# Reordering VectorE in the attention stage of a Performer-attention + MoE kernel, and starting the first expert weights two steps later

## The chip, the cores and the metric

The kernel runs on one core of a Trainium2 chip. The metric is the device time of one execution in microseconds (us), the median over runs. One execution was also taken by the hardware profiler; its span starts and ends with the program's instructions and is a little shorter than the execution's device time.

Five engines have a queue of instructions each and run side by side: PE (TensorE, matrix products), DVE (VectorE), ACT (ScalarE), POOL (GpSimd) and SP (SyncE, which here only issues transfers). Within a queue instructions go strictly in the order of the program.

## The reference

```python
# attention with random features: q, k, v are (2, 8, 576, 64), omega is (128, 64)
scale = 1 / sqrt(sqrt(64))
def phi(x):                       # x = q * scale or k * scale
    proj = einsum('bhsd,md->bhsm', x, omega)
    sq = sum(x * x, -1) / 2
    h = proj - sq
    h = h - max(h, -1)
    return exp(h) / sqrt(128)
kv = einsum('bhsm,bhsd->bhmd', k_p, v); z = sum(k_p, axis=2)
out = (q_p @ kv) / (q_p @ z + 1e-6)
# then x (1152 tokens x 512) goes through a mixture of 4 experts of width 1024
# (relu(x @ w1[e]) @ w2[e], weighted by normalised probabilities), and through
# h = x @ w_in (512 x 2048); (h * cos(h)) @ w_out (2048 x 512)
```

## The kernel before, in words

**Two streams of work.** The attention is done by pairs of heads: 2 batches x 4 pairs give `NPR` = 8 pairs of 512 tokens each, and one more "tail" that holds the last 64 tokens of every head. A loop `for s in range(NPR + 3)` (line 1257) runs the pairs as a software pipeline. The dense work (experts and the last two layers) is a Python generator `stream`, cut into quanta of 6 or 12 matmuls. `dense_quanta` (L1186) lets one quantum into the loop at four places of a step, but only from step `first` = 6 on. Before step 6 the loop holds attention alone. After the loop the rest of the stream runs by itself.

**One step of the loop.** What stands in step `s`, in the order in which it is written out (each engine keeps this order):

- `kv_of(s - 1)`: 8 matmuls of features of keys with v (tile `kv`, L1074), added to the tail's share on DVE (L1078);
- `turn_phi(s - 1)`: the features of queries `phq` are turned by PE (`tq`, L1087) and copied out of PSUM to `pT`, one half by ACT (L1090), one by DVE (L1092);
- `put_x` of pair `s - 2`: PE turns the attention result `xs` (`tx`, L1035), ACT writes its high part `xh` (L1047), DVE the low part `xl` = value - `xh` (L1049);
- `features` of queries of pair `s` and then of keys of pair `s + 1`: PE projects (`pj_q`, `pj_k`, L985). DVE sums the squares (L992), scales the sum (L993), takes the maxima of the two projections (L998, twice) and makes the bias `nb_q` or `nb_k` (L1003, L1006). ACT takes 8 exponentials with this bias (`phq`, `phk`, L1011);
- `norms_ahead`: POOL squares the next queries and keys (L941) and halves the row three times by adding (L945), into `x2`;
- `turn_ahead(s + 1)`: PE turns the next queries and keys (`tp_q`, `tp_k`, L958), and they are copied out of PSUM: `xT_q` on DVE (L969), `xT_k` on ACT (L967);
- `nums(s - 1)`: PE forms numerators and denominators (`num`, L1103), DVE divides (L1023 to L1027) into `xs`;
- transfers of later pairs on SP's queue (`load_k`, `load_q`, `load_v`).

**The first weights.** The eight pieces of weights that the first expert needs first are read in the loop: `load_a(0, u, "p")` for four pieces of `w1` (`p0` to `p3`, buffers `ra_..`), and `load_v2(0, u)` for four of `w2` (`v0` to `v3`, buffers `rv`). Each is split into a high part (ACT, L129, 128x1024) and a low part (POOL, L134, two instructions). One piece is fetched per step from step 0 on (L1318), and its split comes about two steps later (`wait(2)`). The raw pieces share two buffers (pool `raw`), so a fetch waits until POOL has split the piece before the last one, and SP's queue stands behind that wait.

**PSUM.** All PSUM tiles rotate through 8 banks; a matmul into a new tile waits until the last reader of the bank's earlier tile is done.

Of the kernel before, what the change touches and what calls it, by code (L numbers as in the profile page):

```python
# [13 lines left out]
ALU = mybir.AluOpType  # L14
# [12 lines left out]
def performer_moe_kernel(ctx, tc, q, k, v, omega, probs, w1, w2, w_in, w_out, out):  # L27
    nc = tc.nc
# [336 lines left out]
    def advance(under):  # L365

        for g in list(under):
            if next(g, under) is under:
                under.remove(g)
# [504 lines left out]
    with tc.tile_pool(name="at1", bufs=1) as at1, tc.tile_pool(name="at2", bufs=2) as at2:  # L874
# [63 lines left out]
        def norms_ahead(nm, t):  # L938

            x2 = at2.tile([P, 2 * R, D], F32, tag=f"x2{nm[0]}", name=f"x2_{nm}")  # L940
            nc.gpsimd.tensor_tensor(out=x2, in0=t, in1=t, op=ALU.mult)  # L941
            w = D
            while w > 8:
                w //= 2
                nc.gpsimd.tensor_tensor(  # L945
                    out=x2[:, :, 0:w], in0=x2[:, :, 0:w], in1=x2[:, :, w : 2 * w], op=ALU.add
                )
            sqs[nm] = x2[:, :, 0:w]

        def turn(nm, t, pieces=1):  # L950

            n = R // pieces
            tps = []
            for z in range(pieces):
                tp = bank(f"tp_{nm}_{z}")[:, : n * P]
                tps.append((slice(z * n * P, (z + 1) * n * P), tp))
                for i in range(n):
                    nc.tensor.transpose(  # L958
                        tp[:, i * P : (i + 1) * P], t[:, 2 * (z * n + i) : 2 * (z * n + i) + 2, :], ident
                    )  # L960

            def copy(x=None, x2=None, act=True):
                if x is None:
                    x = at2.tile([P, R * P], F32, tag=f"xT{nm[0]}", name=f"xT_{nm}")
                for z, (c, tp) in enumerate(tps):
                    if act and z == (nm[0] == "q"):
                        nc.scalar.activation(x[:, c], tp, ACTF.Copy)  # L967
                    else:
                        nc.vector.tensor_copy(out=x[:, c], in_=tp)  # L969
                    if x2 is not None:  # L970
                        nc.scalar.activation(x2[:, c], tp, ACTF.Square)
                return x

            return copy

        def features(nm, turned, phi, squares=None):

            nb = at2.tile([P, 2 * R], F32, tag=f"nb{nm}"[:3], name=f"nb_{nm}")
            pjs = [bank(f"pj_{nm}_{g}") for g in range(2)]
            for i in range(R):  # L980
                c = slice(i * P, (i + 1) * P)
                for z, (x_, y) in enumerate([(turned, ws)] + [(squares, minus_norm)] * (squares is not None)):
                    for g, pj in enumerate(pjs):
                        r = slice(g * D, (g + 1) * D)
                        nc.tensor.matmul(  # L985
                            pj[:, i * M : (i + 1) * M], x_[r, c], y[r, :],
                            start=z == 0, stop=z == (squares is not None),
                        )
            yield
            three = at2.tile([P, 2 * R, 3], F32, tag=f"th{nm[0]}", name=f"three_{nm}")  # L990
            if squares is None:
                nc.vector.tensor_reduce(out=nb, in_=sqs.pop(nm), op=ALU.add, axis=AX.X)  # L992
                nc.vector.tensor_scalar(  # L993
                    out=three[:, :, 1], in0=nb, scalar1=-SC * SC / 2, scalar2=None, op0=ALU.mult
                )
            for g, pj in enumerate(pjs):
                to = (nb if squares is not None else three[:, :, 0])[:, g : 2 * R : 2]
                nc.vector.tensor_reduce(  # L998
                    out=to, in_=pj.rearrange("p (a m) -> p a m", m=M), op=ALU.max, axis=AX.X,
                    negate=squares is not None,  # L1000
                )
            if squares is None:
                nc.vector.tensor_reduce(  # L1003
                    out=three[:, :, 2], in_=three[:, :, 0:2], op=ALU.add, axis=AX.X, negate=True
                )
                nc.vector.tensor_reduce(out=nb, in_=three[:, :, 1:3], op=ALU.add, axis=AX.X)  # L1006
            yield
            for g, pj in enumerate(pjs):
                for i in range(4):
                    ix = g + 2 * i  # L1010
                    nc.scalar.activation(  # L1011
                        phi[:, ix, :], pj[:, i * M : (i + 1) * M], ACTF.Exp, bias=nb[:, ix : ix + 1]
                    )
                yield
# [16 lines left out]
        def put_x(nm, kk, xs, t0, n):  # L1031

            tp = bank(f"tx_{nm}")
            for i in range(n):
                nc.tensor.transpose(tp[:, i * P : (i + 1) * P], xs[:, i, :, :], ident)  # L1035
            yield
            to, i0 = [], 0
            while i0 < n:
                c, o = divmod(t0 + i0, TC)
                m_ = min(n - i0, TC - o)  # L1040
                d = slice(o * HALF, (o + m_ - 1) * HALF + 1, HALF) if c == 0 else (
                    slice(where(c).start + o, where(c).start + o + m_)
                )
                to.append((as_tiles(tp[:, i0 * P : (i0 + m_) * P]), *(x[:, kk, d, :] for x in x_t)))
                i0 += m_
            for src, xh, xl in to:
                nc.scalar.activation(xh, src, ACTF.Copy)  # L1047
            for src, xh, xl in to:
                nc.vector.tensor_tensor(out=xl, in0=src, in1=xh.bitcast(F32), op=ALU.subtract)  # L1049

# [131 lines left out]

        first = 6
        budget = [0.0]

        def dense_quanta(s, n):  # L1186
            if s < first:
# [4 lines left out]
                next(stream)  # L1192

        DQ = 1.0
        wload = []
        turned = {}

        def q_of(s):
# [24 lines left out]
        warm(1)  # L1223
        q0 = turn("q0", qts[0])
        warm(1)
        turned["k", 0], turned["q", 0] = k0(), q0()
        xkL = at2.tile([P, R * P], F32, tag="pT0", bufs=1, name="xkL")
        x2L = at2.tile([P, R * P], F32, tag="pT1", bufs=1, name="x2L")
        phiL = at1.tile([P, H, M], F32, name="phiL")
# [27 lines left out]
        for s in range(NPR + 3):  # L1257
            if s == 0:
                load_k(3)
                load_q(2)  # L1260
                load_v(1)
            else:
                if s < first:
                    advance(wload)
                dense_quanta(s, DQ)
                kvs = kv_of(s - 1) if s <= NPR else iter(())
                next(kvs, None)
                if s == 1:
                    turn_phi(0)
                    kv_tail(phiL)  # L1270
                next(kvs, None)
                if s >= first:
                    advance(wload)
                dense_quanta(s, DQ)
                if 2 <= s <= NPR:
                    turn_phi(s - 1)
                elif s == NPR + 1:
                    tail_turn_phi()
                px = iter(())
                if 2 <= s <= NPR + 1:  # L1280
                    b, hp = pairs[s - 2]
                    px = put_x(f"{s - 2}", hp, xss.pop(s - 2), b * R, R)
                elif s == NPR + 2:
                    px = tail_put_x()
                next(px, None)
                for _ in px:
                    pass
                fs = []
                if s <= NPR:
                    fs.append(q_features(s))  # L1290
                if s + 1 < NPR:
                    fs.append(k_features(s + 1))
                for f in fs:
                    next(f)
                for f in fs:
                    next(f)
                dense_quanta(s, DQ)
                for f in fs:
                    for _ in f:
                        pass  # L1300
                if s + 1 <= NPR:
                    norms_ahead(f"q{s + 1}", q_of(s + 1))
                if s + 2 < NPR:
                    norms_ahead(f"k{s + 2}", kts[s + 2])
                turn_ahead(s + 1)
                dense_quanta(s, DQ)
                if s <= NPR:
                    nums(s - 1)
                elif s == NPR + 1:
                    tail_nums()  # L1310
                if s + 3 < NPR:
                    load_k(s + 3)
                if s + 2 < NPR:
                    load_q(s + 2)
                if s + 1 < NPR:
                    load_v(s + 1)
            advance(wload)
            if s < 2 * NU:  # L1318
                wload.append(load_a(0, s, "p") if s < NU else load_v2(0, s % NU))
                advance(wload)  # L1320
            if s == 2:
                nc.vector.tensor_reduce(out=psum_, in_=pr, op=ALU.add, axis=AX.X)
            if s == 4:
# [44 lines left out]
```

## Time and profile before

| | us |
|---|---|
| median of 3 runs | 664.62 (662.21 to 665.06) |
| the profiled execution, device time | 663.72 |
| its span | 661.9 |
| PE busy | 651.8 (98%) |
| DVE / ACT / POOL busy | 495.6 / 355.5 / 170.7 |
| first dense matmul of the loop starts at | 64.15 |

A busy PE is not a fast PE: its clock has two levels, and the profile gives the granted clock of each stretch as a share of the full one. In the stretch without dense work (the first 64 us) PE is slower than in the rest or waits; what it waits for there is the matter of the rows below. Times of one execution differ from the median by some tenths of a per cent.

### The profile page before, as it was taken

The numbers are of one execution on the slowest core, as the hardware profiler recorded it, in microseconds if no ns is written. First come the engines' busy times: TensorE is split into PE (matmuls) and PEld (weight loads), VectorE is DVE, ScalarE is ACT, GpSimd is POOL, SyncE is SP. The second block draws the span as 40 slices with busy tenths as digits, with TensorE's granted clock in tenths as the row PEclk, the third lists the DMA queues.
The fourth block names the chain that finished last, engine by engine and source line by source line (L and its number), as shares of the span: only waits on it lengthen the run. The fifth ranks groups of instructions, "written<-read, shape, count | busy, mean of one in ns | idle before, by whom it ended". The sixth has DMA issues, their size and how long they took to land.

```text
span 661.9 us, 9631 instructions
## 1 busy us (share of the span) xinstructions
PE 651.8 (98%) x3495; PEld 565.5 (85%) x3495; DVE 495.6 (75%) x916; ACT 355.5 (54%) x703; POOL 170.7 (26%) x220
## 2 busy tenths in 40 slices
PE   9898999999999999999999999999999999999997
PEld 8898998998888888888888888888999888888887
DVE  6868657778969767679778688698778676497842
ACT  6676655436645445345444254464376884467921
POOL 8768544203333232323333322220000000000000
PEclk9988999999999999999999999999999999999999
DMA  7743212131444533435534344420801000700111
GB/s 188 199 128 96 51 64 63 54 107 64 149 151 147 184 134 128 127 128 159 191 100 147 119 145 161 156 79 17 318 32 33 1 0 24 294 1 1 48 49 48
DMA packets 55439, 70.93 MB, mean 107 GB/s; under 512 B 15200, under 2 KB 40032, under 8 KB 55392
## 3 DMA queue, kind: packets, MB, share of 16 engines
q1 hardware_dynamic: 46800, 40.92, 20.0%
q0 software_dynamic: 8448, 29.37, 13.0%
q8 instruction: 27, 0.44, 0.3%
q14 instruction: 20, 0.16, 0.1%
q10 hardware_dynamic: 144, 0.03, 0.0%
HBM read 55.36 MB, written 14.94 MB: 106 GB/s over the span
## 4 chain that ended last, share of the span: by engine, by line
PE 86%; DVE 6%; ACT 3%; issue 2%; DMA 1%; POOL 1%; ACTq 0%; DVEq 0%; POOLq 0%
PE g L704 43%; PE g L503 5%; PE g_odd L533 3%; PE g_0a L503 2%; PE g_0c L503 2%; PE g_3a L503 2%; PE g_2a L503 2%; PE g_1a L503 2%; PE g_2c L503 2%; PE g_3c L503 2%; PE g_1c L503 2%; PE kv L1074 2%; PE g_0b L503 1%; PE g_0e L503 1%; PE g_0d L503 1%
## 5 line engine op out<-in xcount | busy, mean ns | idle before, releaser
L674 ACT ACTIVATE sth<-h 128x512 fp32r<-128x512 f32 (+1 forms) x114 | 61.0, 551 | 66.4 <-PE g L704 51.5
L248 POOL TENSOR_TENSOR c<-c 128x512 uint32<-128x512 uint32 x32 | 46.7, 1458 | 83.8 <-issue 29.1
L677 DVE SCALAR_TENSOR_TENSOR stl<-h,sth 128x512 fp32r<-128x512 f32 (+1 forms) x72 | 50.3, 717 | 20.9 <-ACT sth L674 20.5
L704 PE MATMUL g<-v3h,sth 128*128 128x512 f32 (+1 forms) x110 | 42.8, 390 | 0.0
L704 PE MATMUL g<-v0h,stl 128*128 128x512 f32 (+1 forms) x110 | 42.6, 387 | 0.1
L704 PE MATMUL g<-v1h,sth 128*128 128x512 f32 (+1 forms) x110 | 42.7, 388 | 0.0
L704 PE MATMUL g<-v2h,sth 128*128 128x512 f32 (+1 forms) x110 | 42.6, 387 | 0.0
L704 PE MATMUL g<-v0h,sth 128*128 128x512 f32 (+1 forms) x110 | 42.6, 387 | 0.0
L704 PE MATMUL g<-v2h,stl 128*128 128x512 f32 (+1 forms) x110 | 42.5, 387 | 0.0
L704 PE MATMUL g<-v1h,stl 128*128 128x512 f32 (+1 forms) x110 | 42.4, 386 | 0.0
L704 PE MATMUL g<-v3h,stl 128*128 128x512 f32 (+1 forms) x110 | 42.4, 386 | 0.0
L704 PE MATMUL g<-v0l,sth 128*128 128x512 f32 (+1 forms) x110 | 42.4, 386 | 0.0
L704 PE MATMUL g<-v1l,sth 128*128 128x512 f32 (+1 forms) x110 | 42.4, 385 | 0.0
L704 PE MATMUL g<-v3l,sth 128*128 128x512 f32 (+1 forms) x110 | 42.4, 385 | 0.0
L704 PE MATMUL g<-v2l,sth 128*128 128x512 f32 (+1 forms) x110 | 42.4, 385 | 0.0
L282 DVE TENSOR_TENSOR stl<-h,sth 128x512 fp32r<-128x512 f32 (+1 forms) x42 | 24.4, 588 | 21.1 <-ACT sth L674 20.7
L1011 ACT ACTIVATE phq<-pj_q,nb_q 128x128 f32<-128x128 f32 x72 | 19.6, 383 | 24.6 <-DVE nb_q L1006 14.7
L403 DVE SCALAR_TENSOR_TENSOR c<-c 128x384 f32<-128x384 f32 (+2 forms) x44 | 25.8, 591 | 9.0 <-ACT c L401 8.8
L233 ACT ACTIVATE c<-c 128x512 f32<-128x512 f32 x32 | 21.1, 660 | 17.1 <-DMA kv_0h<-c 8.8
L232 ACT ACTIVATE c<-c 128x512 f32<-128x512 uint32 x32 | 21.3, 666 | 8.5 <-DMA c<-in_moe_w_in_dram 7.5
L401 ACT ACTIVATE c<-c 128x384 f32<-128x384 f32 (+2 forms) x44 | 24.4, 555 | 1.4
L704 PEld LDWEIGHTS g<-v0h,stl 128*128 128x128 f32 x110 | 20.7, 188 | 4.9 <-DVE stl L677 0.7
(416 smaller groups left out, 1941.2 us busy)
## 6 DMA issues: line engine op xcount, KB each, us to landing
rv<-in_moe_w_dram SPq DMA_DIRECT2D x16, 512.0 KB, 3.8
c<-in_moe_w_in_dram POOLq DMA_DIRECT2D x16, 512.0 KB, 4.2
c<-in_moe_w_out_dram POOLq DMA_DIRECT2D x16, 512.0 KB, 3.8
kt<-in_k_dram SPq DMA_DIRECT2D x8, 256.0 KB, 3.8
qt<-in_q_dram SPq DMA_DIRECT2D x8, 256.0 KB, 4.0
ve<-in_v_dram SPq DMA_DIRECT2D x16, 128.0 KB, 3.8
ra_2as<-in_moe_w_dram SPq DMA_DIRECT2D x8, 256.0 KB, 3.0
ra_3as<-in_moe_w_dram SPq DMA_DIRECT2D x8, 256.0 KB, 3.7
```

Source lines behind the costliest of these rows:

```text
L232: nc.scalar.activation(lw.bitcast(F32), lw, ACTF.Copy, bias=2.0, scale=2.0**-51)
L233: nc.scalar.activation(t.bitcast(F32), hw.bitcast(F32), ACTF.Abs)
L248: nc.gpsimd.tensor_tensor(out=total, in0=t, in1=lw, op=ALU.add)
L282: nc.vector.tensor_tensor(out=dst, in0=x, in1=y, op=ALU.subtract)
L401: nc.scalar.activation(kk, vv, ACTF.Copy, bias=ROUND)
L403: nc.vector.scalar_tensor_tensor(out=vv, in0=kk, scalar=ROUND, in1=vv, op0=ALU.subtract, op1=ALU.subtract)
L503: nc.tensor.matmul(dst, x[:, o], y[:, kk], start=start and n == 0, stop=stop and n == 3 * kn - 1, skip_group_check=reopen,)
L533: nc.tensor.matmul(g, x[:, kk], w[:, :, :, kk, :], start=n == 0, stop=n == 3 * KD - 1)
L674: nc.scalar.activation(hi, src, ACTF.Relu if self.e < E else ACTF.Copy)
L677: nc.vector.scalar_tensor_tensor(out=to, in0=src, scalar=0.0, in1=hi.bitcast(F32), op0=ALU.max, op1=ALU.subtract)
L704: nc.tensor.matmul(g, x, y[:, o : o + w], start=n == 0, stop=n == 3 * FT - 1)
L1011: nc.scalar.activation(phi[:, ix, :], pj[:, i * M : (i + 1) * M], ACTF.Exp, bias=nb[:, ix : ix + 1])
```

## The change

Five edits, all in the attention loop and ahead of it:

1. `features`: the sums of squares are scaled on POOL, in `norms_ahead`, instead of on DVE (L993 goes; a new POOL instruction of 128x8x8 for each of 17 tiles).
2. `turn`: `xT_q` is copied by ACT instead of DVE (except for the first two pairs, which pass `act=False`).
3. `put_x` yields between ACT's `xh` and DVE's `xl`, and the loop puts `xl` behind the maxima and the bias of queries, ahead of those of keys.
4. The first weights are fetched at the end of steps 2 (`p0`), 3 (`p1`), 4 (`p2`), 5 (`p3` and `v0`), 6 (`v1`, `v2`) and 7 (`v3`), instead of one a step in steps 0 to 7.
5. `q0` keeps its copy on DVE by an argument.

```diff
@@ norms_ahead
+            nc.gpsimd.tensor_scalar(
+                out=x2[:, :, 0:w], in0=x2[:, :, 0:w], scalar1=-SC * SC / 2, scalar2=None, op0=ALU.mult
+            )
             sqs[nm] = x2[:, :, 0:w]
@@ turn
-                    if act and z == (nm[0] == "q"):
+                    if act and (z == 0 or nm[0] == "q"):
                         nc.scalar.activation(x[:, c], tp, ACTF.Copy)
                     else:
                         nc.vector.tensor_copy(out=x[:, c], in_=tp)
@@ features
-                nc.vector.tensor_reduce(out=nb, in_=sqs.pop(nm), op=ALU.add, axis=AX.X)
-                nc.vector.tensor_scalar(
-                    out=three[:, :, 1], in0=nb, scalar1=-SC * SC / 2, scalar2=None, op0=ALU.mult
-                )
+                nc.vector.tensor_reduce(out=three[:, :, 1], in_=sqs.pop(nm), op=ALU.add, axis=AX.X)
@@ put_x
             for src, xh, xl in to:
                 nc.scalar.activation(xh, src, ACTF.Copy)
+            yield
             for src, xh, xl in to:
                 nc.vector.tensor_tensor(out=xl, in0=src, in1=xh.bitcast(F32), op=ALU.subtract)
@@ the loop
+        fetched = {2: [("p", 0)], 3: [("p", 1)], 4: [("p", 2)], 5: [("p", 3), ("v", 0)]}
+        fetched.update({6: [("v", 1), ("v", 2)], 7: [("v", 3)]})
...
-        turned["k", 0], turned["q", 0] = k0(), q0()
+        turned["k", 0], turned["q", 0] = k0(), q0(act=False)
...
                 next(px, None)
-                for _ in px:
-                    pass
+                next(px, None)
...
                 for f in fs:
                     next(f)
-                for f in fs:
+                for f in fs[:1]:
+                    next(f)
+                for _ in px:
+                    pass
+                for f in fs[1:]:
                     next(f)
...
-            if s < 2 * NU:
-                wload.append(load_a(0, s, "p") if s < NU else load_v2(0, s % NU))
-                advance(wload)
+            for kind, u in fetched.get(s, ()):
+                wload.append(load_a(0, u, "p") if kind == "p" else load_v2(0, u))
+                next(wload[-1])
```

**VectorE, step 3.** Before, from the addition of `kv` to the bias of queries (`tq`, `tx`, `pj` are PSUM tiles, numbers are the tiles' own):

```order
L1078 TENSOR_TENSOR kv_142<-kv_662,kvL_146 128x2x65
L1092 COPY pT_1_684<-tq_1_679 128x512
L1049 TENSOR_TENSOR xl<-tx_686,xh 128x3x128
L1049 TENSOR_TENSOR xl<-tx_686,xh 128x128
L992 TENSOR_REDUCE nb_q_697<-x_q_606 128x8
L993 TENSOR_SCALAR three_q_719<-nb_q_697 128x8
L998 TENSOR_REDUCE three_q_719<-pj_q_0_698 128x4
L998 TENSOR_REDUCE three_q_719<-pj_q_1_699 128x4
L1003 TENSOR_REDUCE three_q_719<-three_q_719 128x8
L1006 TENSOR_REDUCE nb_q_697<-three_q_719 128x8
```

In the change the same stretch of VectorE's queue reads:

```order
L1079 TENSOR_TENSOR kv_142<-kv_652,kvL_146 128x2x65
L1093 COPY pT_1_674<-tq_1_669 128x512
L995 TENSOR_REDUCE three_q_707<-x_q_597 128x8
L998 TENSOR_REDUCE three_q_707<-pj_q_0_686 128x4
L998 TENSOR_REDUCE three_q_707<-pj_q_1_687 128x4
L1003 TENSOR_REDUCE three_q_707<-three_q_707 128x8
L1006 TENSOR_REDUCE nb_q_685<-three_q_707 128x8
L1050 TENSOR_TENSOR xl<-tx_676,xh 128x3x128
L1050 TENSOR_TENSOR xl<-tx_676,xh 128x128
L995 TENSOR_REDUCE three_k_715<-x_k_603 128x8
```

The two `xl` instructions went from ahead of the maxima of queries to behind their bias, and the scaling is gone.

**ScalarE, from the exponentials of keys in step 2 to those of queries in step 3.** Before (`w02h` is the high part of the weight piece `p1`):

```order
L1011 ACTIVATE phk_553<-pj_k_1_567,nb_k_565 128x128 x4
L967 ACTIVATE xT_k_628<-tp_k_0_621 128x512
L129 ACTIVATE w02h<-ra_1p 128x1024
L1090 ACTIVATE pT_0_677<-tq_0_672 128x512
L1047 ACTIVATE xh<-tx_686 128x3x128
L1047 ACTIVATE xh<-tx_686 128x128
L1011 ACTIVATE phq_695<-pj_q_0_698,nb_q_697 128x128 x4
```

In the change the same stretch of ScalarE's queue reads:

```order
L1011 ACTIVATE phk_544<-pj_k_1_558,nb_k_556 128x128 x4
L970 ACTIVATE xT_q_619<-tp_q_0_609 128x512
L970 ACTIVATE xT_k_621<-tp_k_0_614 128x512
L1091 ACTIVATE pT_0_667<-tq_0_662 128x512
L1047 ACTIVATE xh<-tx_676 128x3x128
L1047 ACTIVATE xh<-tx_676 128x128
L1011 ACTIVATE phq_683<-pj_q_0_686,nb_q_685 128x128 x4
```

The copy of the turned queries came in behind the exponentials of keys, and the split of weights left this step (`p0` is split in step 4 now, `p1` in step 5, `p2` in step 6, `p3` and `v0` in step 7, `v1` and `v2` in step 8).

**SyncE, the fetches of step 5's end and after.** In the change SP's queue has, from the fetch of the last queries on:

```order
L911 DMA qt_3_1067<-in_q_dram 128x2x256
L920 DMA ve_133<-in_v_dram 128x4x64 x2
L160 DMA ra_3p<-in_moe_w_dram 128x4x128 x2
L138 DMA rv_0_1075<-in_moe_w_dram 128x2x512
L920 DMA ve_134<-in_v_dram 128x4x64 x2
L138 DMA rv_1_1228<-in_moe_w_dram 128x2x512
L138 DMA rv_2_1230<-in_moe_w_dram 128x2x512
```

Two fetches of weights stand together twice here; before, a fetch of queries, keys or v stood between any two of the first seven pieces.

## Rows read from the trace of the kernel before

**Rows 1.** Windows: length; PE, PEld, DVE, ACT, POOL busy (instructions); PE's granted clock; DMA.

```profile
33.00:38.00 5.00, 5.00 (x25) 5.00 (x26) 2.25 (x11) 4.58 (x13) 2.73 (x5) 0.50 0.52 148
43.50:52.10 8.60, 8.24 (x86) 7.60 (x85) 6.19 (x19) 5.63 (x17) 4.77 (x6) 1.00 0.34 93
...
64.15:661.90 597.75, 593.59 (x2944) 511.01 (x2944) 448.83 (x780) 314.65 (x575) 123.36 (x144) 1.00 0.31 102
```

**Rows 2.** The timeline, 21 to 32 us, ACT and DVE (start, length, instruction, idle before).

```profile
21.30 2.18 ACT L1011 ACTIVATE phq<-pj_q,nb_q 128x128 f32<-128x128 f32 x8 [2.52 <-DVE nb_q L1006]
...
23.32 2.23 ACT L1011 ACTIVATE phk<-pj_k,nb_k 128x128 f32<-128x128 f32 x8
...
25.32 0.71 ACT L967 ACTIVATE xT_k<-tp_k 128x512 f32<-128x512 f32 x1
...
25.80 1.18 ACT L129 ACTIVATE w02h<-ra_0p 128x1024 fp32r<-128x1024 f32 x1
...
26.75 0.72 ACT L1090 ACTIVATE pT<-tq 128x512 f32<-128x512 f32 x1
...
28.05 0.76 DVE L1049 TENSOR_TENSOR xl<-tx,xh 128x384 fp32r<-128x384 f32 x2 [1.90 <-ACT xh L1047]
...
28.72 0.21 DVE L992 TENSOR_REDUCE nb_q<-x_q 128x8 f32<-128x64 f32 x1
28.96 0.63 DVE L993 TENSOR_SCALAR three_q<-nb_q 128x8 f32<-128x8 f32 x1
29.51 1.28 DVE L998 TENSOR_REDUCE three_q<-pj_q 128x4 f32<-128x512 f32 x2
...
31.02 0.17 DVE L1006 TENSOR_REDUCE nb_q<-three_q 128x8 f32<-128x16 f32 x1
...
31.31 2.18 ACT L1011 ACTIVATE phq<-pj_q,nb_q 128x128 f32<-128x128 f32 x8 [3.29 <-DVE nb_k L992]
```

**Rows 3.** The timeline: the next steps' first exponentials of queries, and the first dense matmul.

```profile
42.30 2.18 ACT L1011 ACTIVATE phq<-pj_q,nb_q 128x128 f32<-128x128 f32 x8 [2.86 <-DVE nb_q L1006]
...
52.94 2.18 ACT L1011 ACTIVATE phq<-pj_q,nb_q 128x128 f32<-128x128 f32 x8 [3.29 <-DVE nb_k L992]
...
62.95 2.18 ACT L1011 ACTIVATE phq<-pj_q,nb_q 128x128 f32<-128x128 f32 x8 [3.20 <-PE num L1103]
...
64.15 0.45 PE L503 MATMUL g<-xh,w02h 128*128 128x384 f32 x1 [0.34 <-ACT phq L1011]
```

**Rows 4.** The timeline on PE: `kv` after a wait, a step's `pj_q` and `num`, `pj_q` later.

```profile
32.51 3.68 PE L1074 MATMUL kv<-ve,phk 128*128 128x65 f32 x16 [1.91 <-ACT phq L1011]
...
47.28 1.16 PE L985 MATMUL pj_q<-ws,xT_q 64*128 64x128 f32 x16
...
50.20 1.90 PE L1103 MATMUL num<-kv,pT 128*128 128x65 f32 x16
...
54.14 2.00 PE L1074 MATMUL kv<-ve,phk 128*128 128x65 f32 x16 [2.04 <-ACT phq L1011]
...
69.56 1.16 PE L985 MATMUL pj_q<-ws,xT_q 64*128 64x128 f32 x16
...
81.31 1.16 PE L985 MATMUL pj_q<-ws,xT_q 64*128 64x128 f32 x16
```

**Rows 5.** Single lines of DVE over the whole run: count, ns shortest/median/longest.

```profile
L993 DVE TENSOR_SCALAR three_q<-nb_q x9: 173/535/966, 9.7 to 93.8; 128x8 f32<-128x8 f32 x9
...
L992 DVE TENSOR_REDUCE nb_q<-x_q x9: 208/208/221, 9.4 to 93.6; 128x8 f32<-128x64 f32 x9
```

**Rows 6.** The chain that ended last, ahead of step 1 (start, length, what).

```profile
9.09 0.33 POOL x_q L945
...
9.70 0.74 DVE three_q L993
```

**Rows 7.** The timeline: a low part on POOL; and the page's transfers (KB, us to landing).

```profile
27.06 2.50 POOL L134 TENSOR_TENSOR w02l<-ra_0p,w02h 128x512 fp32r<-128x512 f32 x2 [3.96 <-DMA ve<-in_v_dram]
...
rv<-in_moe_w_dram SPq DMA_DIRECT2D x16, 512.0 KB, 3.8
```

More of the change, by code (lines that the diff above doesn't have):

```diff
@@ L1184, in performer_moe_kernel @@
         budget = [0.0]
+        wload = []
+        fetched = {2: [("p", 0)], 3: [("p", 1)], 4: [("p", 2)], 5: [("p", 3), ("v", 0)]}
+        fetched.update({6: [("v", 1), ("v", 2)], 7: [("v", 3)]})
         def dense_quanta(s, n):
@@ L1194, in performer_moe_kernel @@
         DQ = 1.0
-        wload = []
         turned = {}
```

## The prediction

> **What bounds the kernel now.** I began with the windows. From the first dense matmul at 64.15 to the end PE is busy 593.59 of 597.75 us at full clock, so little can be won there. Ahead of it lies the attention part, and there a window (33 to 38) calls PE busy at a granted clock of 0.50, that is 1.2 GHz in place of 2.4 [rows 1]. What stands behind 64.15 is a fixed queue of matmuls; it ends earlier by as much as it begins earlier, as long as nothing new makes it wait. The question is what sets 64.15.
>
> It is a loop from step to step. I take the first exponential of queries (`phq`) as the mark of a step: 21.30 and 31.31 [rows 2], then 42.30, 52.94 and 62.95 [rows 3], so steps 1 to 4 take 10.01, 10.99, 10.64 and 10.01 us, 41.65 in all. The timeline of the first of them shows the order of starts [rows 2]: ACT does `phq` for 2.02 (21.30 to 23.32), `phk` for 2.00, then one after the other `xT_k`, the split `w02h`, `pT` and `xh`. Only then can DVE begin `xl` (it had waited 1.90 for ACT), and behind `xl` stand the sum of squares, its scaling and the maxima of queries, whose bias releases the next `phq`; ACT sat idle 3.29 until it came. ACT's jobs and DVE's chain follow each other instead of overlapping. PE is not the limit: the window from 43.50, where a `kv` begins, to 52.10, where the step's last `num` ends, holds a whole step's matmuls and is 8.60 long, 8.24 of it busy, at full clock [rows 1, 4]. PE waits for the exponentials instead: 1.91 us ahead of one `kv`, 2.04 ahead of another [rows 4].
>
> The clock makes it worse. Behind the wait of 1.91 the granted clock is 0.50, and the 16 matmuls of `kv` take 3.68 us, where they take 2.00 elsewhere [rows 1, 4]; that step is the longest of the four.
>
> **The change part by part.** *`xl` behind the queries' bias, and the copy on ACT.* In the new loop, from mark to mark: `phq` 2.02, `phk` 2.00, then `xT_q` stands first on ACT; it takes what `xT_k` took, 0.71 [rows 2]. When it is done, PE projects the queries, 1.16 for `pj_q` [rows 4]. Then come the maxima of queries; from their start to the next `phq` it is 29.51 to 31.31, 1.80 [rows 2]. The sum of squares is done before that, while DVE waits. Together 7.69 us. From step 2 on `xl` stands between the bias of queries and the maxima of keys, so `phk` begins later. From the start of the queries' bias, 0.29 ahead of the mark, DVE needs about 0.1 for itself, 0.67 for `xl` (28.05 to 28.72), 0.24 for the sum (to 28.96), and 1.80 again for the keys' maxima and bias: `phk` starts 2.5 after the mark, not 2.02, which is 0.49 more and makes **8.18 us** [rows 2].
>
> The rest of ACT's work must fit beside that. Between `phk` and the next `phq` stand `xT_q` and `xT_k` (0.48 each by their starts) and `pT` and `xh` (1.30 from the start of `pT` to `xl`), 2.26 of the 3.67 us that PE and DVE need meanwhile; the split, 0.95 by starts, comes back in step 4 and fits too [rows 2]. If it did not, a step with a split would be up to 0.95 longer.
>
> Step 1 has no `xl`: 7.69. Steps 2 to 4 at 8.18 are 24.54. Together 32.2 for 41.65: **-9.4 us**.
>
> *PE in that loop.* Its matmuls, 8.24 busy, stand against 8.18. I count them as just hidden, because the window's busy time includes waits inside merged rows; if 8.60 is the limit, steps 2 to 4 cost 0.42 more each and step 1 0.9, 2.2 us.
>
> *Scaling on POOL.* On DVE the scaling of eight numbers a row took 173 to 966 ns, median 535 [rows 5]; in the loop it goes with the sums above. Ahead of step 1 the first queries' sum waits for POOL, so there the new instruction counts twice (keys, then queries), against 0.74 of scaling on the path [rows 6]. No row shows this instruction. Below it could be next to nothing; above, one of the two instructions of a low part, 1.25 at eight times its columns [rows 7]; the nearest row is the last halving of the sum, 0.33 on the same 64 columns [rows 6], and I take that: 2 x 0.33 - 0.74 = -0.1. The scalings of `k1` and `q1` lie in a busy stretch of DVE and give at least their shortest time, 0.173 each [rows 5], -0.3. **-0.4 us** (-1.0 at nothing, +1.5 at 1.25). In later steps the squares are made a step ahead, which hides the instruction; without that cover two of them would lengthen each step, 0.7.
>
> *Start of the dense part.* The first dense matmul stands behind `num` on PE. From the end of `pj_q` (48.44) to the end of `num` (52.10) PE needs 3.66 [rows 4]. The mark comes 1.80 after the end of `pj_q`, so `num` ends 1.9 behind the mark, where the dense part began 1.20 behind it before (62.95 to 64.15) [rows 3]. **+0.7 us.**
>
> *Weights two steps later.* ACT has the same 8 splits, but they meet a date: `p3` is split in step 7 and used there behind `pj_q`. Counted from the mark of step 6: `phk` is over at 4.5, `xT_q` at 5.0, one evacuation of a dense tile (about like `pT`, 0.48) at 5.5, the high part at 6.7 (1.18), POOL's low part at 9.2 (2.50) [rows 2, 7]. PE, bound by its own queue there, ends `pj_q` of step 7 at 9.95 (11.75 after that of step 6, which is 1.80 ahead of the mark [rows 4]). So about 0.7 us are to spare. **0**; without that cover PE stands for what is missing, 1 to 3 us.
>
> The sum: -9.4 - 0.4 + 0.7 = **-9.1**. The profiled execution took 663.72, its span 661.9; that gives 654.6. The median of the runs, 664.62, is 0.9 above the profiled execution, so I predict **655.5 us**.
>
> **A page weighed against the rows.** The scaling that is removed took 0.63 at 28.96 while POOL's low part ran from 27.06 to 29.56 [rows 2, 7]; the sums of squares never took more than 221 ns in nine cases [rows 5]. So the stretch goes with the scaling and does not pass to the sum that now stands in its place. If it passed, about 0.4 (535 - 173 ns) in four steps and ahead of them, 2 us of the 9.1 would be gone. The Trainium skill (SBUF — State Buffer, section "SBUF: two separate sides") says that VectorE and GpSimd hold one port pair exclusively, which binds VectorE instructions in a two-port mode or with two SBUF inputs, and that the loser waits for the whole instruction. By that rule one-input sums outside such a mode stay free, as the rows say, and the sum stays -9.1.
>
> **The rivals.** *The clock falls as before.* For it: PE has a small gap in every new step, about half a us until `xT_q` is done. Against it: the window from 43.50 has 0.36 without work and a granted clock of 1.00; the fall came behind 1.91 [rows 1, 4]. The longest step shows the price, 10.99 against 10.01, about 1 us; in all four steps 4, so 659.5. The Trainium skill (TensorE: Matmul & The Clock Gate, Part 1, "The HAM clock gate") has the array throttled by default and released by activity; the trace agrees, with 0.50 behind that wait and 1.00 in the dense part. Chance 0.12.
>
> *Smaller terms go against me*: PE's matmuls as the limit (2.2), the stretch passed on (2), a dear POOL instruction (1.9). One or two of them: 657 to 659.5. Chance 0.14.
>
> *The gain is given back*: the dense part starts earlier but waits for its first weights by as much. For it: splits are now packed into steps 4 to 8, two in each of steps 7 and 8, with 0.7 us to spare at one place. Against it: a landing of 3.8 us [rows 7] against steps of 8 to 12. It needs a delay of 6 to 12 us: 661.5 to 667, call it 664. Chance 0.07.
>
> *Slower.* One mechanism: ACT's queue is held by the high part of `v0`. Its fetch waits on SP until POOL has freed the raw buffer of `p2`, split in step 6; ACT reaches it in step 7 ahead of `pT`, `xh` and the next `phq`, and all stand behind it. POOL frees the buffer about 9.5 behind the mark of step 5, and ACT comes 6.7 behind that of step 6, which is some 10 us after it, so 7 us later; the landing takes 3.8 [rows 7], so 3 are to spare. Only a landing of 7 begins to cost, one of 16 eats the gain, and from 20 us on it is slower by 0.5%: 668. Chance 0.03.
>
> **How the numbers follow.** My forecast holds 0.64, with a range of its own from 653.5 to 657. About 0.5%, 3.3 us, is what a measurement of this kernel can tell from no change; below 661.3 is faster. The forecast, the smaller terms and most of the clock's case lie there, 0.88; the gain given back and what is left of the clock's case make 0.08 same; slower is 0.04, with 0.01 from the upper end of the gain given back. The range goes from 652.5, where POOL's instruction costs nothing and the steps are 0.4 shorter, to 660, which takes in the smaller terms and the clock.
>
> **What would show it.** Marks 8.2 us apart in steps 2 to 4, the first dense matmul at about 55, a granted clock of 1.00 in all windows of the loop, no wait of 1.9 for `xh` ahead of `xl`, and ACT's idle time ahead of `phq` down to 1.4 where no split stands. Wrong it would be if a window ahead of 55 shows 0.50, if PE waits in steps 6 to 9 for `w3l` or a `v` piece, or if marks stay 10 apart.

## The result and the profile after

The changed kernel takes **654.9 us** (median; 654.76 to 655.47) where the kernel before took 662.92 in the same runs (662.03 to 665.06): ratio 0.9875, 95% interval 0.9856 to 0.9893, so 1.25% faster. The prediction was 655.5 us, and its sum for the profiled execution 654.6; that execution took 654.85 (span 652.7). The profiled execution of the kernel before, 663.72, lies 0.8 above the median of its runs, so what the two traces differ by (spans 661.9 and 652.7, 9.2 us) is more than the 8.0 us between the medians. One execution of the kernel before, among those that belong to the four "only" kernels below, took 930.53 us at a mean granted clock of 0.654, a slow state of the chip, and is left out of all medians and ratios.

The time came from the loop. In the timeline of the changed kernel, the marks (the first `phq` of a step) and the first dense matmul; rows 2 and 3 answer to them [rows 2, 3]:

```profile
21.22 2.18 ACT L1011 ACTIVATE phq<-pj_q,nb_q 128x128 f32<-128x128 f32 x8 [2.44 <-DVE nb_q L1006]
...
29.07 2.18 ACT L1011 ACTIVATE phq<-pj_q,nb_q 128x128 f32<-128x128 f32 x8 [1.59 <-DVE nb_q L1006]
...
37.16 2.18 ACT L1011 ACTIVATE phq<-pj_q,nb_q 128x128 f32<-128x128 f32 x8 [1.53 <-DVE nb_q L1006]
...
45.26 2.17 ACT L1011 ACTIVATE phq<-pj_q,nb_q 128x128 f32<-128x128 f32 x8 [0.59 <-DVE nb_q L1006]
...
53.35 2.18 ACT L1011 ACTIVATE phq<-pj_q,nb_q 128x128 f32<-128x128 f32 x8 [0.49 <-DVE nb_q L1006]
...
54.96 0.42 PE L503 MATMUL g<-xh,w02h 128*128 128x384 f32 x1
```

Steps 1 to 4 take 7.85, 8.09, 8.10 and 8.09 us, 32.13 in all instead of 41.65. The dense part starts at 54.96 instead of 64.15, 9.19 earlier, and the windows show that it is otherwise what it was: 597.74 us now, 597.75 before [rows 1]. In the stretch 20 to 66 the granted clock is 1.00 throughout; in the same window of the kernel before it was 0.89, with 41.36 us busy. The windows (length; PE, PEld, DVE, ACT, POOL busy; granted clock; DMA), first of the kernel before:

```profile
20.00:66.00 46.00, 41.36 (x373) 39.22 (x374) 34.26 (x109) 30.33 (x98) 32.20 (x44) 0.89 0.47 131
```

and of the changed kernel:

```profile
20.00:66.00 46.00, 45.46 (x464) 43.60 (x461) 33.52 (x110) 37.49 (x120) 38.47 (x59) 1.00 0.45 126
...
54.96:652.70 597.74, 593.39 (x2946) 511.17 (x2945) 445.50 (x773) 318.11 (x579) 132.28 (x157) 1.00 0.32 104
```

What closes the loop now is read in the chain that ended last, here one step of it, from `xl` of step 2 to `xl` of step 3:

```profile
28.95 0.66 DVE xl L1050 x2
29.61 0.13 DVE three_k L995
29.74 1.21 DVE three_k L998 x2
...
31.17 0.17 DVE nb_k L1006
31.34 0.08 DVE rd L1023
...
31.44 1.71 ACT phk L1011 x7
...
33.62 0.49 ACT xT_q L970
...
34.16 1.21 PE pj_q L988 x16
35.37 1.28 DVE three_q L998 x2
...
36.88 0.17 DVE nb_q L1006
37.04 0.66 DVE xl L1050 x2
```

`xh`, `pT` and `phq` are no longer in it; ACT does them beside it. It runs over the copy that the change put on ACT (`xT_q`) and over `xl` ahead of the maxima of keys, as the prediction's sum of 8.18 had it.

### The profile page after: what moved, and what is told of

Same layout as the page of the kernel before. It is cut to its first block, busy times and chain, and to the rows that moved or that the text cites. A ratio compares the mean times of both kernels' runs of the same rounds, so it can differ in the third digit from the quotient of the medians.

```text
span 652.7 us, 9626 instructions
## 1 busy us (share of the span) xinstructions
PE 646.7 (99%) x3495; PEld 561.7 (86%) x3495; DVE 484.9 (74%) x892; ACT 359.3 (55%) x710; POOL 176.9 (27%) x237
## 4 chain that ended last, share of the span: by engine, by line
PE 90%; DVE 5%; issue 2%; ACT 2%; DMA 1%; POOL 0%; DVEq 0%; ACTq 0%; POOLq 0%
PE g L704 44%; PE g L503 5%; PE g_odd L533 3%; PE g_0a L503 2%; PE g_0c L503 2%; PE g_3a L503 2%; PE g_2c L503 2%; PE g_2a L503 2%; PE g_1a L503 2%; PE g_3c L503 2%; PE g_1c L503 2%; PE pj_q L988 2%; PE kv L1075 1%; PE num L1104 1%; PE g_0b L503 1%
```

## The experiments

Each part was run alone on the kernel before ("only"), and each was taken out of the changed kernel ("less"). Time is the median with its range; steps 1 to 4 are the distances of the marks in the profiled execution. The two kernels themselves are in the first two rows; the steps of before are those of the rows ahead of the prediction [rows 2, 3]. Each ratio goes by runs of before in between: their median is 663.30 us for the four "only" kernels, 662.35 for the four "less", 662.26 for the last three.

| kernel | us | ratio to before, 95% | steps 1 to 4 | dense part from |
|---|---|---|---|---|
| before | 662.92 (662.03–665.06) | 1 | 10.01 10.99 10.64 10.01 | 64.15 |
| changed | 654.90 (654.76–655.47) | 0.9875 (0.9856–0.9893) | 7.85 8.09 8.10 8.09 | 54.96 |
| only_order | 654.72 (654.55–655.16) | 0.9873 (0.9853–0.9894) | 7.44 7.86 7.91 7.95 | 55.83 |
| only_weights | 659.62 (659.24–660.33) | 0.9944 (0.9922–0.9966) | 8.82 8.59 9.99 9.98 | 60.11 |
| only_copy | 664.92 (663.34–666.71) | 1.0023 (1.0007–1.0038) | 10.53 10.49 10.47 10.55 | 65.45 |
| only_scaling | 661.25 (659.32–664.31) | 0.9970 (0.9951–0.9989) | 9.33 9.48 9.34 9.43 | 59.89 |
| less_order | 659.87 (659.17–663.71) | 0.9960 (0.9943–0.9977) | 8.88 8.87 9.83 10.68 | 61.03 |
| less_weights | 655.11 (654.55–655.80) | 0.9885 (0.9857–0.9913) | 7.85 8.09 8.09 8.09 | 55.29 |
| less_copy | 654.39 (654.21–654.64) | 0.9874 (0.9846–0.9901) | 7.84 7.84 7.85 7.84 | 54.50 |
| less_scaling | 655.57 (654.81–655.81) | 0.9889 (0.9862–0.9917) | 8.11 8.29 8.29 8.39 | 56.12 |
| clock_fill | 662.04 (661.73–663.55) | 0.9998 (0.9989–1.0007) | 10.00 9.98 9.99 9.99 | 62.87 |
| xl_last | 656.88 (656.14–657.40) | 0.9920 (0.9907–0.9934) | 7.84 8.48 8.48 8.48 | 56.61 |
| pe_more | 657.98 (657.90–658.17) | 0.9935 (0.9923–0.9948) | 8.73 8.74 8.74 8.74 | 58.79 |

**Theory:** the gain is the loop ACT → `xl` → maxima → ACT, which the order of `xl` breaks. **Rival:** it is the work taken off DVE, ACT's splits moved away and the clock, each with its share.

**only_order.** `put_x` (which now yields between `xh` and `xl`) and the loop as in the change, the rest as before:

```diff
+            yield
...
-                for _ in px:
-                    pass
+                next(px, None)
...
-                for f in fs:
+                for f in fs[:1]:
+                    next(f)
+                for _ in px:
+                    pass
+                for f in fs[1:]:
                     next(f)
```

> The kernel before with the third edit alone: xl behind the bias of queries. Theory (the loop ACT, then xl, then maxima was the bound, and the order breaks it): marks about 8.0 to 8.4 us apart, since pj_q no longer waits for the copy of the turned queries (VectorE has it early), ACT's seven jobs with the split (7.4) fit beside it, and the scaling of keys' sums stays on the way to phk; first dense matmul near 56.5, -7.5 us on the kernel before, granted clock 1.00. Rival (work taken off ScalarE and VectorE is what gains): -2 us at most, marks still near 9.5 or more.

This part alone gives the whole gain, 654.72, with the marks closer than I had expected (7.44 to 7.95). In the built program the loop's PSUM tiles have the same banks as in the kernel before up to step 3, so there the order is all that differs. PE is then the limit: in its timeline one `kv` follows the other after 7.85 us, without an idle time ahead of it:

```profile
32.15 1.95 PE L1075 MATMUL kv<-ve,phk 128*128 128x65 f32 x16
...
40.00 1.95 PE L1075 MATMUL kv<-ve,phk 128*128 128x65 f32 x16
```

**only_weights, only_copy, only_scaling.** The weights' schedule alone (`fetched`), the copy alone (`act and (z == 0 or nm[0] == "q")` with `act=False` for `q0`), and the scaling alone:

> The kernel before with the fourth edit alone: first weights two steps later. Theory: the loop stays, ScalarE has 0.95 less in the first two steps and the same later, -1.9 us, and maybe 1 more if one fall of the clock goes. Rival (weights out of the way are the main gain): -5 us or more.

> The kernel before with the second edit alone: xT_q copied by ScalarE. Theory: ScalarE is in the loop, so each step grows by 0.48, +1.9 us, and pj_q comes later. Rival (VectorE is the bound and is relieved by 0.68 a step): -2 us.

> The kernel before with the first edit alone: the scaling of sums on GpSimd. Theory: what the scaling held on the path goes, 0.55, 0.11, 0.54 and 0.45 from its start to the maxima of queries in steps 1 to 4 and about 0.7 once ahead of phk: -2.3 us, nothing in the part ahead of step 1. Rival (the stretch passes to another instruction): 0.

With the weights moved, steps 1 and 2, which lost their splits, fall to 8.82 and 8.59, but a window at 52 to 54 still has PE at 0.50; the gain, 3.7 us, was larger than the 1.9 to 2.9 I had said. One part that I had not counted: without the low part on POOL, the scaling of step 1 takes 0.17 us and not 0.63. The copy alone makes the kernel slower, by 0.07% to 0.38% (1.6 us by the medians): it makes ACT's half of the loop longer, to 10.5 us a step. The scaling alone shortens each step, yet the time fell by 2.1 us only. Its dense part starts at 59.89 after PE waited 1.37 us for ACT, and its clock is down to 0.53 in the window from 60 to 64 (it is 0.50 from 64 to 66 and 1.00 again from 68 on):

```profile
60.00:64.00 4.00, 4.00 (x18) 4.00 (x18) 1.94 (x9) 4.00 (x14) 3.50 (x7) 0.53 0.12 48
```

The rest took 660.8 - 59.89 = 600.9 us instead of 597.75 [rows 1], so 3 us of what the loop gave came back. Alone the three are worth 3.7, -1.6 and 2.1 us; what they are worth beside the order, the next four show.

**less_order, less_weights, less_copy, less_scaling.** The changed kernel without one part each:

> The changed kernel without the third edit: xl again ahead of the maxima of queries. Theory (the order carries the gain): the loop is back with phq 2.02, phk 2.00, xT_q 0.48, xT_k 0.48, pT 0.48, xh 0.8, xl 0.67, sum 0.13 and maxima 1.80, that is 8.9 us a step and 9.8 in the two with a split, 5.4 us slower than the changed kernel, near 660.3. Rival (the other three edits carry it): within 2 us of the changed kernel, near 656.

> The changed kernel with the first weights fetched one a step from step 0 on, as before. Theory: the split fits beside PE's and VectorE's chain (ScalarE still idled 0.5 ahead of phq in the steps that have it), so 0, near 655. Rival: 0.95 in each of the first two steps, 656.8.

> The changed kernel with xT_q copied by VectorE again. Theory by the same chain: pj_q no longer waits for a copy behind phk but for tx, which waits for xs on VectorE, now 0.7 later: marks about 7.9 apart instead of 8.09, -0.6 us, so 654.3 or no difference. Rival (the copy on ScalarE is needed): +0.68 a step, 657.6.

> The changed kernel with the scaling on VectorE again. Theory: the queries' scaling hides in the 0.95 us that VectorE waits for pj_q, but that of the keys' sums stands on the way to phk and costs 0.1 to 0.9 a step: +1 to +2 us, near 656.4. Rival: hidden as well, 0.

Without the order the other parts leave 659.87, so beside them the order is worth 5.0 us: the loop is back, as this kernel's timeline on DVE shows, where `xl` waits for `xh` and the maxima of queries stand behind `xl`:

```profile
36.31 0.76 DVE L1049 TENSOR_TENSOR xl<-tx,xh 128x384 fp32r<-128x384 f32 x2 [1.47 <-ACT xh L1047]
36.98 0.21 DVE L995 TENSOR_REDUCE three_q<-x_q 128x8 f32<-128x64 f32 x1
37.11 1.28 DVE L998 TENSOR_REDUCE three_q<-pj_q 128x4 f32<-128x512 f32 x2
```

In the changed kernel the maxima stand ahead, and wait for PE instead:

```profile
34.18 0.21 DVE L995 TENSOR_REDUCE three_q<-x_q 128x8 f32<-128x64 f32 x1
35.35 1.29 DVE L998 TENSOR_REDUCE three_q<-pj_q 128x4 f32<-128x512 f32 x2 [0.96 <-PE pj_q L988]
...
36.88 0.17 DVE L1006 TENSOR_REDUCE nb_q<-three_q 128x8 f32<-128x16 f32 x1
36.96 0.74 DVE L1050 TENSOR_TENSOR xl<-tx,xh 128x384 fp32r<-128x384 f32 x2
```

Beside the order the weights are worth 0.2 us by the medians, the copy -0.5 and the scaling 0.7 (less than the 1 to 2 us that I expected). The changed kernel was timed in another round; by the ratios it is 0.7, -0.1 and 0.9, and the intervals of all three ratios overlap with the changed kernel's, so the times do not show a gain or a loss for any of the three. The marks are clearer: without the copy all steps take 7.84 and the dense part starts 0.46 earlier; without the scaling on POOL steps take up to 8.39.

**pe_more.** less_copy, with one half of `num` issued twice in the first five pairs:

```diff
-                for r in range(R):
+                for r in list(range(R)) * (2 if i < 5 and h == 0 else 1):
                     nc.tensor.matmul(
                         num[:, r * (D + 1) : (r + 1) * (D + 1)], pT[:, r * P : (r + 1) * P],
```

> The changed kernel without the copy of xT_q on ACT, and one half of the matmuls of num issued twice in the first five pairs (same output; 0.87 us more of PE work in each of steps 1 to 5). Theory: PE's matmuls are the floor of a step (7.84 us by the starts of kv, without a wait), so the steps go to 8.71 and the first dense matmul comes 4.3 us later: about 658.7. Rival: another chain is as long as PE's work by chance and PE has room; steps of 7.9 to 8.1 and under 655.5.

The steps grew by 0.89, about PE's added work, and the dense part starts at 58.79, 4.29 later than in less_copy; the median rose by 3.6 (654.39 to 657.98). So in less_copy PE's own matmuls are the floor. The windows, of less_copy and of pe_more:

```profile
20.00:66.00 46.00, 46.00 (x473) 44.36 (x471) 37.15 (x117) 35.58 (x116) 38.80 (x60) 1.00 0.47 127
```

```profile
20.00:66.00 46.00, 46.00 (x480) 44.52 (x476) 33.29 (x106) 33.29 (x105) 37.35 (x58) 1.00 0.44 125
```

**clock_fill.** The kernel before, with both halves of `num` issued twice (`2 if i < 5 else 1`), which fills the waits ahead of `kv`:

> The kernel before, with the matmuls of num issued twice in the first five pairs (same output; 1.73 us more of PE work in each of steps 1 to 5, put where PE waits 1.9 to 2.0 us for the exponentials of keys ahead of kv). Theory: before, part of the lost time is the clock, which falls to 0.50 behind those waits; with the waits filled no window before the dense part shows 0.50, steps 2 and 3 (10.99 and 10.64 us) come down to the 10.0 of the others, and the first dense matmul comes 1 to 1.6 us earlier: 0.998 of before, although PE does 8.7 us more work. First rival: the waits are not what lowers the clock; it falls as before and the time stays or rises by up to 1 us. Second rival: the added matmuls delay xs and so the next step's chain; steps of 11 to 12 us and about +5 us.

Half right. No window shows 0.50 any more, PE is busy without a pause, and with 5 x 1.73 = 8.7 us more of work its dense part still starts 1.28 earlier; but the runs show no gain: the ratio is 0.9998, and my 0.998 lies outside its interval. The steps are 10.00, 9.98, 9.99 and 9.99, while PE starts a `kv` every 9.63 us and waits for nothing:

```profile
34.01 1.95 PE L1074 MATMUL kv<-ve,phk 128*128 128x65 f32 x16
...
41.28 2.17 ACT L1011 ACTIVATE phq<-pj_q,nb_q 128x128 f32<-128x128 f32 x8 [3.29 <-DVE nb_k L992]
...
43.64 1.95 PE L1074 MATMUL kv<-ve,phk 128*128 128x65 f32 x16
```

So the loop of ACT and DVE alone sets 10 us, and PE's doubled `num` hides in it. What the falls of the clock cost beyond that in the profiled execution of the kernel before is 1.7 us (41.65 - 39.96), and the medians do not show it. The cost differs from one execution to the next: of the 55 executions of the kernel before in the three rounds of experiments, the 30 with a mean granted clock of 0.994 or 0.995 took 661.34 to 663.22 us, the 25 with 0.987 to 0.992 took 662.93 to 667.34. The profiled one had 0.992, but 11 of the 15 beside clock_fill had 0.994 or 0.995. One word of the expectation was wrong: the trace names the exponentials of queries as what `kv` waited for [rows 4]. They read `pj_q`, whose PSUM bank this `kv` takes over in the built program. The window on clock_fill:

```profile
20.00:62.87 42.87, 42.87 (x440) 41.71 (x441) 32.63 (x102) 28.62 (x92) 30.91 (x42) 1.00 0.52 140
```

**xl_last.** The changed kernel with `xl` behind the maxima of keys as well:

```diff
-                for f in fs[:1]:
+                for f in fs:
                     next(f)
                 for _ in px:
                     pass
-                for f in fs[1:]:
-                    next(f)
```

> The changed kernel with xl behind the maxima of keys too, not between those of queries and keys. Theory, by the step I summed for the prediction: xl ahead of the keys' maxima makes phk start 0.4 to 0.5 us later, and with it xT_q and pj_q; without it the loop of ACT, PE and DVE takes 7.69, PE's own 7.84 are then the limit, steps 2 to 4 take 7.84 in place of 8.09, and the time is about 0.7 us under that of the changed kernel (654.2), as in the kernel without the copy on ACT (654.4). Rival: xT_q on ACT itself costs the 0.25, wherever xl stands; steps of 8.1 and 654.9.

Neither: it is slower than the changed kernel, by 2.0 us by the medians and 3.0 by the ratios. `phk` does start sooner, 2.01 behind the mark instead of 2.37, but PE waits at a new place. In its timeline the second half of `num` waits for the first exponentials of queries:

```profile
28.86 1.00 PE L1104 MATMUL num<-kv,pT 128*128 128x65 f32 x8
...
28.95 2.17 ACT L1011 ACTIVATE phq<-pj_q,nb_q 128x128 f32<-128x128 f32 x8 [1.61 <-DVE nb_q L1006]
...
30.15 1.10 PE L1104 MATMUL num<-kv,pT 128*128 128x65 f32 x8 [0.28 <-ACT phq L1011]
...
31.18 2.00 PE L1075 MATMUL kv<-ve,phk 128*128 128x65 f32 x16
```

In steps 2 to 4 the chain that ended last runs from the first exponentials of queries over this half of `num`, `kv`, `tq`, `tx`, `pj_q` and the maxima to the next mark, 8.48 us. `num` computes nothing from `phq` of this step; what they share is PSUM. In the built programs the bank of this `num` is that of `tx` in the changed kernel, and in xl_last that of `pj_q`, which the exponentials read. `xl` is the last reader of `tx`; where it comes earlier in the program, the bank of `tx` is free to be handed on first. So `xl` has a latest place too. That the bank is the cause is read from the programs and the wait; no run held the banks fixed.

## Why the prediction was right

**What bounds the kernel.** Right. ACT's jobs and DVE's chain followed each other; only_order breaks that by the order alone, and takes 8.6 us of 663.3 away, the whole gain. clock_fill shows from the other side that PE did not set the 10 us.

**The loop, -9.4.** Measured -9.5 (32.13 for 41.65). Steps 2 to 4 were summed as 8.18 and are 8.09: `phk` begins 2.37 behind the mark, not 2.5. Step 1 was summed as 7.69 and is 7.85, because PE has its own floor there.

**PE "just hidden".** Right, but with more room than I thought: I left the limit between 8.24 and 8.60, and it is 7.84 (less_copy, only_order, pe_more), under the 8.09 of the chain. The reason that I gave for the room, waits inside merged rows, is not what the rows show. The window holds one pause, 0.35 ahead of `tx`, which is the 0.36 without work, and busy time counts a group's last matmul to its end even where nothing follows: `num` is 1.90 long at the window's end [rows 4] and `tq` 1.04 ahead of the pause, while in less_copy the next group starts 1.73 and 0.88 after their starts. These two make 0.33 of the 0.4.

**The copy on ACT.** I counted it inside the 8.18 and did not price it by itself. By the marks it is a loss of 0.25 a step, which the times are too coarse to show: PE waits 0.18 for it ahead of `pj_q` in the timeline of the changed kernel, and 8.09 falls to 7.84 without it:

```profile
42.25 1.16 PE L988 MATMUL pj_q<-ws,xT_q 64*128 64x128 f32 x16 [0.18 <-ACT xT_q L970]
```

**Scaling and the first steps, -0.4.** Measured -0.08 (first mark 21.22, before 21.30): a mis-sized term. POOL's instruction takes 0.37 to 0.38, where I had 0.33, and the next one starts 0.45 after it; it counts twice. DVE's sum for the first queries waits 1.12 for POOL, and the maxima behind it start at 10.63, where before they started at 10.35. The scalings of the second pair give back 0.36. The timeline of the changed kernel:

```profile
6.77 0.38 POOL L948 TENSOR_SCALAR x_k<-x_k 128x64 f32<-128x64 f32 x1
...
10.09 0.37 POOL L948 TENSOR_SCALAR x_q<-x_q 128x64 f32<-128x64 f32 x1
...
10.49 0.22 DVE L995 TENSOR_REDUCE three_q<-x_q 128x8 f32<-128x64 f32 x1 [1.12 <-POOL x_q L948]
```

**Start of the dense part, +0.7.** Measured +0.41 (1.61 behind the mark, before 1.20). The sum of all three terms was -9.1; measured in the traces are -9.2.

**From the profiled execution to the median, +0.9.** This did not come true. The +0.9 came from the first three runs of the kernel before; over its six runs the median, 662.92, is 0.8 below the profiled execution, and the changed kernel's median is 0.05 above its own. So this term, which had no mechanism behind it, puts 655.5 above the measured 654.9; the sum for the profiled execution was 0.25 too low, and that the two errors partly cancel is luck. That the trace gains 9.2 and the medians 8.0 fits the clock: by their times and clocks (see clock_fill) more than half of the executions of the kernel before lost less to it than the profiled one, and the six of the changed kernel have 0.999 or 1.000. It is not shown beyond that.

**The stretch goes with the scaling.** Right: the sums of squares now take 208 to 222 ns in all 17 cases. The rule on VectorE's and GpSimd's shared ports, as the prediction read it from the Trainium skill (SBUF — State Buffer, section "SBUF: two separate sides"), agrees with that.

**The weights, 0.** Right: no PE wait for a piece of weights in the changed kernel from 20 to 120, and less_weights differs by 0.2 by the medians. The rival in which they give the gain back did not come true, nor did the one of `v0`.

**The clock's rival.** It did not come true. PE's longest wait in the loop is 0.18 now, and the granted clock stays at 1.00. The five kernels in which it fell to 0.50 to 0.53 have waits of 1.4 to 2.1 us ahead of a `kv` or of the dense part (before 2.0, only_weights 1.9, only_copy 2.1, only_scaling 1.4, less_order 1.4); in the others the longest is 0.5 (only_order, less_scaling).

## What to carry to other kernels

When an engine that is far from full sets the time, follow the loop through the queues from one step's mark to the next and look for the instruction that waits for another engine while something ready, which that engine needs, stands behind it; moving this one behind gave all 8 us by itself here, and the three edits that only move work between engines or steps are worth next to nothing beside it. Then ask what the next floor is (here PE's own 7.84 us a step) and leave out edits that only shorten what already lies under it. Moving a reader of PSUM back can also change which bank the next tiles get, so look for new waits of PE on tiles that it doesn't use.

## What the runs showed that I had not expected

The gains of parts don't add: alone they give 8.6, 3.7, -1.6 and 2.1 us, 13 in sum, and 8.0 together. Where two parts act on the same loop, the price of each depends on what else is in it.

A small VectorE instruction next to GpSimd can move the whole first part: in only_order, where the scaling stays on DVE, two of the scalings ahead of step 1 took 1.04 and 0.98 us, and the first mark stands at 23.06 instead of 21.30. In its timeline, with what POOL does:

```profile
14.80 1.04 POOL L941 TENSOR_TENSOR x_k<-kt 128x512 f32<-128x512 f32 x1
14.83 1.04 DVE L993 TENSOR_SCALAR three_k<-nb_k 128x8 f32<-128x8 f32 x1
...
20.27 1.04 POOL L941 TENSOR_TENSOR x_k<-kt 128x512 f32<-128x512 f32 x1
20.36 0.98 DVE L993 TENSOR_SCALAR three_q<-nb_q 128x8 f32<-128x8 f32 x1
```

The step after that was 7.44, under PE's floor, so part of it was made up at once. Each of the two began just behind the start of POOL's 1.04 us instruction and ended 0.03 after its end. The kernel before shows the same: all nine of its 17 scalings that take more than 0.18 us end 0.01 to 0.04 after a POOL instruction that was running when they began. There the first of the two began at 14.59, ahead of that long instruction, and took 0.33; in only_order DVE came 0.23 later to the reduction ahead of it (`nb_kL`, 12.18 for 11.95), because PE's first projections ended later. 0.23, 0.71 for the first scaling and 0.81 for the second (0.17 before) are the 1.76 of the mark, to 0.01. Why PE was later there is open.
